# Gated linear attention into a four-expert MLP: crossbar transposes replaced by TensorE transposes, and the first gate logits loaded from ACT's queue

## The chip, the cores and the metric

One core of one Trainium2 chip. The metric is the device time of one execution in microseconds (us), as the median of several runs. Three runs of the kernel before took 315.59, 315.67 and 315.96 us.

The engines are named as in the profile: PE is TensorE (PEld its weight loads), DVE VectorE, ACT ScalarE, POOL GpSimd, and SP the engine whose queue issues most DMAs here.

## What is computed

Two stages. The first is a linear attention with a per-channel forget gate over 4 batches, 8 heads, 768 steps and 48 channels a head:

```python
f = 1.0 / (1.0 + np.exp(-f_logit))
for t in range(S):
    state = f[:, :, t, :, None] * state + np.einsum('bhd,bhe->bhde', k[:, :, t], v[:, :, t])
    y[:, :, t] = np.einsum('bhd,bhde->bhe', q[:, :, t], state)
```

The second takes y as 3072 rows of 384 values (rows by batch and step, columns by head and channel) through four experts, each 384 to 1024 to 384 with a ReLU between, and adds the experts' results with weights p, which are the domain probabilities divided by their sum:

```python
for e in range(E):
    h = np.maximum(x @ w1[e], 0.0)
    out += p[:, e:e + 1] * (h @ w2[e])
```

## The kernel before, in words

The sequence is cut into 6 chunks (c = 0 to 5) of 128 steps. For each chunk the attention is done for 4 batches (b), all 8 heads at once, and gives 4 x 128 columns of x transposed (xT); the experts then work on these 512 columns together.

**Attention of one batch of one chunk.** ACT turns the gate logits into log gates (lines 236 and 240, two steps). PE makes their running sum along the chunk with a triangular matrix (244; 247 makes the totals of the chunk). ACT takes exponentials of both signs (251, 252, 254). Q and K are multiplied with them (257, "product", on POOL or DVE) and V is cast (261). Q and K are needed with the channel on the partition, so they are transposed; how depends on the chunk:

- chunks 0 and 1: PE transposes (265, `pe_tp`): four for Q and four for K, each 112 columns wide (two heads, padded to 64 each), into PSUM, and DVE copies them to the tile QK (214).
- chunks 2 to 5: one crossbar DMA per batch from SP's queue (269, `dma_tp`), from the padded tile `qk` straight into QK.

PE then makes the scores (280), DVE masks them (284), and PE adds scores times V and, from chunk 1 on, the state's part into y (295, 291). ACT or DVE casts y to bf16 (214, tile yb). This is transposed into xT: in chunks 0 and 1 by three PE transposes (320, `pe_xt`) and a copy by ACT or DVE (212 or 214), in chunks 2 to 5 by one DMA from SP's queue (273, `dma_xt`). Except in the last chunk, PE makes K times V (301), DVE adds it to the state (308), and POOL scales the state by the chunk's gate total and casts it (315, 316).

**Experts.** An "up" group is three matmuls of 512 columns (324), followed by a ReLU on ACT or DVE (332, 330). A "down" group is four matmuls of 384 columns (336); after two of them ACT or DVE scales and adds the result to the output tile (343, 345, 347), which SP stores (351).

**What sets the order.** A small planner (class `Plan`) is given every step with the engines that can do it, a modelled cost on each, a priority, what it depends on and which buffers ("rooms") it takes and frees. It runs through modelled time and starts, on each engine that is free, the ready step of the best priority whose buffers are free. The program is written out in that order, so every engine works strictly in the planned order. Attention of chunk c + 1 is planned among the expert work of chunk c. PSUM has two rooms for up groups, two for down groups and four for everything in the attention.

**Loads.** Each batch of chunk 0 has its own load of f (gate logits), K, Q and V (192 KB each); later chunks load two batches at a time (384 KB). All are issued from SP's queue, in planned order; chunk 0's order is f0 k0 q0 f1 f2 k1 q1 v0 f3 k2 q2 v1 k3 q3 v2 v3 (line 364). The weights, eight transfers of 768 KB, are issued from POOL's queue and wait for K of batch 3 to have landed (227); the gate load that starts chunk 1 waits for the sixth weight transfer (221).

Of the kernel before, what the change touches and what calls it, by code (L numbers as in the profile page):

```python
# [9 lines left out]
BF16 = mybir.dt.bfloat16  # L10
# [87 lines left out]
def kernel(  # L98
# [11 lines left out]
    nc = tc.nc  # L110
    B, H, S, D = q.shape
    assert (B, H, S, D) == (4, 8, 768, 48)
    T = 128
    C = S // T
    HD = H * D
    NP = H // 2
    P2 = 64
    MP = P2 + D
# [5 lines left out]
    engines = {"ACT": nc.scalar, "DVE": nc.vector, "POOL": nc.gpsimd}  # L124
# [4 lines left out]
    wk = ctx.enter_context(tc.tile_pool(name="wk", bufs=1))  # L129
    PS = bass.MemoryType.PSUM  # L130
    ps = ctx.enter_context(tc.tile_pool(name="ps", bufs=1, space=PS))
    rooms = {"ps_h": 2, "ps_o": 2, "ps_t": 4, "f": 4, "q": 4, "k": 4, "v": 4, "ex": 2, "gp": 4, "e": 2, "qk": 7,
             "vb": 7, "egs": 8, "QK": 2, "AT": 2, "yb": 2, "xT": 2, "h": 2, "o": 8}
    P = Plan(rooms)

# [8 lines left out]
    ones = const.tile([T, 1], BF16)  # L144
    nc.gpsimd.memset(ones, 1.0)
    pads = {}
    for nm, nb in (("gp", 2), ("qk", 2)):
        for i in range(rooms[nm]):
            t = pads[nm, i] = const.tile([T, nb, H, P2], BF16, name=f"{nm}{i}")
            nc.vector.memset(t[:, :, :, D:P2], 0.0)  # L150
# [3 lines left out]
        out=mask01, in_=mask01, compare_op=ALU.is_ge, fill=0.0,  # L154
# [5 lines left out]
    for i in range(2):  # L160
        t = const.tile([MP, B, NP, 2 * D], BF16, name=f"sb{i}")
# [11 lines left out]
    for nm, a in (("f", f_logit), ("q", q), ("k", k), ("v", v)):  # L173
        srcs[nm] = a.rearrange("b h (c t) d -> c t (b h) d", t=T)
    ins = {}
# [1 line left out]
    shapes = {  # L177
        "f": ([T, 2 * H, D], FP32), "q": ([T, 2 * H, D], FP32), "k": ([T, 2 * H, D], FP32), "v": ([T, 2 * H, D], FP32),
        "ex": ([T, 2 * H, D], FP32), "e": ([T, 2, HD], FP32), "egs": ([MP, NP], FP32), "vb": ([T, H, D], BF16),
        "QK": ([128, 2, NP, T], BF16), "AT": ([T, 2, NP, T], BF16), "yb": ([T, HD], BF16),  # L180
        "xT": ([128, KD, NT], BF16), "h": ([128, KF, NT], BF16), "o": ([128, Din], FP32),
        "cs": ([T, 512], FP32), "tp": ([MP, 2, NP, T], BF16), "A": ([T, NP, T], FP32), "y": ([T, 512], FP32),
        "KV": ([T, 512], FP32), "xp": ([T, KD, T], BF16), "ps_h": ([128, NT], FP32), "ps_o": ([128, 512], FP32),
# [2 lines left out]
    def tl(kind, *key):  # L186

        if (kind, key) not in tiles:
            room = kind if kind in rooms else "ps_t"
            slot = P.slot[(room, kind) + key if room == "ps_t" else (room,) + key]  # L190
            if room in ("gp", "qk"):
                tiles[kind, key] = pads[room, slot]
            else:
                shape, dt = shapes[kind]
                pool = ps if room.startswith("ps_") else wk
                tiles[kind, key] = pool.tile(shape, dt, name=f"{room}{slot}")
        return tiles[kind, key]
# [6 lines left out]
    def flat(t, i):  # L204
        return t[:, 2 * i:2 * i + 2, :].rearrange("t h d -> t (h d)")

    def hh(b, n=1):
        return slice((b % 2) * H, (b % 2 + n) * H)

    def copy(eng, out, in_):  # L210
        if eng == "ACT":
            nc.scalar.copy(out=out, in_=in_)  # L212
        else:
            engines[eng].tensor_copy(out=out, in_=in_)  # L214


    def load(c, nm, b, n):
        ins[c, nm, b] = nc.sync.dma_start(out=tl(nm, c, b // 2)[:, hh(b, n), :],
                                          in_=srcs[nm][c, :, b * H:(b + n) * H, :])
        if (c, nm, b) == (1, "f", 0):  # L220
            after(ins[c, nm, b], ins["w", 5])
# [32 lines left out]
            nc.scalar.activation(out=tl("egs", c, b), in_=cs[0:MP, HD:HD + NP], func=AF.Exp, scale=-1.0)  # L254

    def product(c, b, j, eng):
        engines[eng].tensor_tensor(out=tl("qk", c, b)[:, j, :, 0:D], in0=tl("qk"[j], c, b // 2)[:, hh(b), :],  # L257
                                   in1=tl("e", c, b)[:, j].rearrange("t (h d) -> t h d", d=D), op=ALU.mult)

    def cast_v(c, b, eng):  # L260
# [1 line left out]

    def pe_tp(c, b, j):
        for i in range(NP):
            nc.tensor.transpose(out=tl("tp", c, b)[:, j, i, :], in_=flat(tl("qk", c, b)[:, j], i)[:, 0:MP],  # L265
                                identity=ident)

    def dma_tp(c, b):
        nc.sync.dma_start_transpose(out=tl("QK", c, b).rearrange("m j i t -> m (j i) t"),
                                    in_=tl("qk", c, b).rearrange("t j h d -> t (j h d)"))  # L270

    def dma_xt(c, b):
        nc.sync.dma_start_transpose(out=tl("xT", c)[:, :, b * T:(b + 1) * T], in_=tl("yb", c, b))

    def pe_at(c, b):
        QK = tl("QK", c, b)
# [10 lines left out]
    def pe_y(c, b):  # L287
        y, AT, vb, QK = tl("y", c, b), tl("AT", c, b), tl("vb", c, b), tl("QK", c, b)
        for i in range(NP):
            if c > 0:  # L290
                nc.tensor.matmul(out=y[:, i * 2 * D:(i + 1) * 2 * D], lhsT=QK[0:MP, 0, i, :],  # L291
                                 rhs=Sb[c % 2][:, b, i, :], start=True, stop=False, skip_group_check=True)
            for r in range(2):
                h = 2 * i + r
                nc.tensor.matmul(out=y[:, h * D:(h + 1) * D], lhsT=AT[:, r, i, :], rhs=vb[:, h, :],  # L295
                                 start=(c == 0), stop=True, skip_group_check=True)

    def pe_kv(c, b):
        kp, vb = tl("qk", c, b)[:, 1], tl("vb", c, b)
        for i in range(NP):  # L300
            nc.tensor.matmul(out=tl("KV", c, b)[0:MP, i * 2 * D:(i + 1) * 2 * D], lhsT=flat(kp, i)[:, 0:MP],  # L301
                             rhs=flat(vb, i), start=True, stop=True)
# [51 lines left out]
    ld = {}  # L354
    nw = [(0, 1), (1, 1), (0, 2), (2, 1), (1, 2), (3, 1), (2, 2), (3, 2)]

    def add_load(c, nm, b, n, prio, deps=()):
        op = P.add(f"ld {nm}{c}.{b}", {"DMA": 1.05 * n}, lambda e: load(c, nm, b, n), prio,
                   deps=deps, takes=[(nm, c, b // 2)], lag=2.0)
        for i in range(n):  # L360
            ld[c, nm, b + i] = op
        return op

    for i, x in enumerate("f0 k0 q0 f1 f2 k1 q1 v0 f3 k2 q2 v1 k3 q3 v2 v3".split()):
        add_load(0, x[0], int(x[1]), 1, -1000 + i)
    pload = P.add("ld p", {"DMA": 0.3}, lambda e: nc.sync.dma_start(
        out=pt, in_=moe_domain_probs.rearrange("(n p) e -> p n e", p=128)), -900, lag=2.0)
# [13 lines left out]
    def attention(c, slot, gran):  # L381
# [10 lines left out]
        for b in range(B):  # L392
# [8 lines left out]
                       takes=[("e", c, b)] + ([("egs", c, b)] if more else []), frees=[pt_("cs")])  # L401
            pe = {"POOL": 1.0, "DVE": 0.56} if c < 2 else {"POOL": 1.0}
            qm = P.add(f"q {c}.{b}", pe, one(product, 0), s(4) - 0.2,
                       deps=[ex, ld[c, "q", b]], takes=[("qk", c, b)], frees=[("q", c, half), ("e", c, b)])
            km = P.add(f"k {c}.{b}", pe, one(product, 1), s(4) - 0.1,
                       deps=[ex, ld[c, "k", b]], takes=[("qk", c, b)], frees=[("k", c, half), ("e", c, b)])
            vb = P.add(f"v {c}.{b}", {"POOL": 0.5, "DVE": 0.36} if c < 2 else {"POOL": 0.5}, one(cast_v), s(4),
                       deps=[ld[c, "v", b]], takes=[("vb", c, b)], frees=[("v", c, half)])
            if c < 2:
                tq = P.add(f"tpq {c}.{b}", {"PE": 0.22}, on(pe_tp, 0), s(4), deps=[qm],  # L410
                           takes=[pt_("tp")], frees=[("qk", c, b)], lag=0.2)
                tk = P.add(f"tpk {c}.{b}", {"PE": 0.22}, on(pe_tp, 1), s(4) + 0.01, deps=[km],
                           takes=[pt_("tp")], frees=[("qk", c, b)], lag=0.2)
                et = P.add(f"ev_tp {c}.{b}", {"DVE": 0.69}, lambda e, b=b: copy(e, tl("QK", c, b)[0:MP], tl("tp", c, b)), s(4) + 0.1,
                           deps=[tq, tk], takes=[("QK", c, b)], frees=[pt_("tp")])
            else:
                et = P.add(f"tp {c}.{b}", {"DMA": 1.8}, on(dma_tp), s(4), deps=[qm, km], takes=[("QK", c, b)],
                           frees=[("qk", c, b)], lag=2.2)
            at = P.add(f"at {c}.{b}", {"PE": 0.35}, on(pe_at), s(7), deps=[et],
                       takes=[pt_("A", 0), pt_("A", 1)], lag=0.2, frees=[("QK", c, b)])  # L420
            eA = [P.add(f"ev_at{r} {c}.{b}", {"DVE": 0.7}, on(ev_at, r), s(7) + 0.1 + 0.1 * r, deps=[at],
# [3 lines left out]
            ey = P.add(f"ev_y {c}.{b}", {"ACT": 0.48, "DVE": 0.56},  # L425
                       lambda e, b=b: copy(e, tl("yb", c, b), tl("y", c, b)[:, 0:HD]), s(11) + 0.1,
                       deps=[y], takes=[("yb", c, b)], frees=[pt_("y")])
            if c < 2:
                xt = P.add(f"xt {c}.{b}", {"PE": 0.17}, on(pe_xt), s(13), deps=[ey],
                           takes=[pt_("xp")], frees=[("yb", c, b)], lag=0.2)  # L430
                xdone[c, b] = P.add(f"ev_xt {c}.{b}", {"ACT": 0.48, "DVE": 0.4},
                                    lambda e, b=b: copy(e, tl("xT", c)[:, :, b * T:(b + 1) * T], tl("xp", c, b)),
                                    s(13) + 0.1, deps=[xt], takes=[("xT", c)], frees=[pt_("xp")])
            else:
                xdone[c, b] = P.add(f"xt {c}.{b}", {"DMA": 0.9}, on(dma_xt), s(13), deps=[ey], takes=[("xT", c)],
                                    frees=[("yb", c, b)], lag=2.2)
            if more:
                kv = P.add(f"kv {c}.{b}", {"PE": 0.22}, on(pe_kv), s(15), deps=[km, vb, y],
                           takes=[pt_("KV")], frees=[("vb", c, b), ("qk", c, b)], lag=0.2)
                ek = P.add(f"ev_kv {c}.{b}", {"DVE": 0.74}, on(ev_kv), s(15) + 0.1,  # L440
                           deps=[kv, kvdone.get((c - 1, b))], frees=[pt_("KV")])
                kvdone[c, b] = P.add(f"state {c}.{b}", {"POOL": 1.75}, on(state), s(15) + 0.2,
                                     deps=[ek, ex], frees=[("egs", c, b)])
# [106 lines left out]
```

## Time and profile before

| what | value |
|---|---|
| median of three runs | 315.67 us |
| profiled execution, its own time | 315.96 us |
| its span, first to last instruction | 314.1 us |
| mean granted TensorE clock | 1.000 |
| first expert matmul starts | 25.38 us |
| end of the last matmul | 310.2 us |
| mean DMA rate over the span | 115 GB/s |

The table's first row is what runs are compared by. The profile is of one execution, whose own time is 0.29 us above that median; its span leaves out 1.86 us around the instructions. A view of busy time by stage gives, for a stretch of the span, how long each engine was busy and how many instructions it ran. In a timeline, each row is a run of equal instructions with start and length in us; rows of PE overlap because matmuls are pipelined, so the distance from one start to the next is what a group costs in a dense stream. "Idle before" names what ended an engine's idle time.

### The profile page before, as it was taken

To read this page: it belongs to the slowest core of one execution; us is meant where nothing else is said; L and a number is where in the kernel's file an instruction comes from. 1 tells how busy PE (TensorE), PEld (TensorE's weight loads), DVE (VectorE), ACT (ScalarE), POOL (GpSimd) and SP (SyncE) were. 2 spreads that over 40 slices of the span, in tenths; PEclk is the share of its full clock that TensorE was granted. 3 is DMA by queue.
4 is the path that set the end of the run, shared out by engine and by line. 5 is a ranking of instruction groups with operands and counts; after the bars stand their busy time and mean duration, and the time that the engine had idled before them with its cause. 6 is when DMAs were issued, how large, how long until landed. Compare 5 with 4: busy or idle time off the path is not lost.

```text
span 314.1 us, 5415 instructions
## 1 busy us (share of the span) xinstructions
PE 295.3 (94%) x2098; PEld 171.1 (54%) x2128; DVE 132.5 (42%) x249; ACT 163.0 (52%) x310; POOL 92.6 (29%) x160
## 2 busy tenths in 40 slices
PE   1978999998999999999999999999999999999995
PEld 1753455556876555655555555555555555555552
DVE  6791002379954466443553222554332442201223
ACT  5634664554767563667544456443466444465430
POOL 4695000026996333860322200223322200000000
PEclk9999999999999999999999999999999999999999
DMA  8999999999999087999692113200322200200002
GB/s 156 211 150 192 196 208 201 208 202 214 189 223 236 6 172 140 230 197 189 108 196 48 50 50 48 46 15 13 95 75 46 50 13 15 75 25 2 0 0 100
DMA packets 135081, 36.05 MB, mean 115 GB/s; under 512 B 126352, under 2 KB 133520, under 8 KB 135056
## 3 DMA queue, kind: packets, MB, share of 16 engines
q1 hardware_dynamic: 129296, 29.42, 49.2%
q0 software_dynamic: 5760, 6.29, 12.0%
q8 instruction: 16, 0.26, 0.4%
q14 instruction: 9, 0.07, 0.1%
HBM read 31.51 MB, written 4.72 MB: 115 GB/s over the span
## 4 chain that ended last, share of the span: by engine, by line
PE 88%; DVE 7%; issue 2%; ACT 1%; DMA 1%; DVEq 0%; ACTq 0%
PE ps_h L324 40%; PE ps_o L336 39%; PE ps_t L280 2%; DVE qk L257 2%; DVE AT L284 2%; PE ps_t L295 1%; PE ps_t L244 1%; PE ps_t L291 1%; PE ps_t L301 1%; PE ps_t L247 1%; DMA f<-in_f_logit_dram 1%; PE ps_t L265 1%; DVE QK L214 1%; DVE o L343 1%; DVE vb L261 1%
## 5 line engine op out<-in xcount | busy, mean ns | idle before, releaser
L332 ACT ACTIVATE h<-ps_h 128x512 bf16<-128x512 f32 (+1 forms) x176 | 101.7, 579 | 111.2 <-PE ps_h L324 104.1
L324 PE MATMUL ps_h<-xT,w_sb 128*128 128x512 bf16 (+1 forms) x594 | 154.0, 367 | 2.9 <-ACT xT L212 0.6
L336 PE MATMUL ps_o<-w_sb,h 128*128 128x384 bf16 x768 | 153.0, 326 | 0.2
L336 PEld LDWEIGHTS <-h 128*128 128x128 bf16 x768 | 72.0, 98 | 56.8
L343 DVE SCALAR_TENSOR_TENSOR o<-ps_o,pn,o 128x384 f32<-128x384 f32 x72 | 44.4, 617 | 109.2 <-PE ps_o L336 101.9
L324 PEld LDWEIGHTS <-w_sb 128*128 128x128 bf16 x624 | 60.5, 99 | 50.9 <-issue 6.5
L284 DVE TENSOR_TENSOR AT<-ps_t,mask 128x512 bf16<-128x512 f32 x48 | 31.2, 684 | 14.8 <-PE ps_t L280 14.7
L261 POOL CAST vb<-v 128x384 bf16<-128x384 f32 x20 | 10.7, 537 | 72.9 <-DMA v<-in_v_dram 36.5
L257 POOL TENSOR_TENSOR qk<-q,e 128x384 bf16<-128x384 f32 x21 | 21.2, 1014 | 30.2 <-ACT e L251 29.9
L315 POOL TENSOR_TENSOR Sf<-Sf,egs 48x192 f32<-48x192 f32 x40 | 20.3, 508 | 24.6 <-DVE Sf L308 22.7
L330 DVE TENSOR_SCALAR h<-ps_h 128x256 bf16<-128x256 f32 (+1 forms) x32 | 17.4, 549 | 23.6 <-PE ps_h L324 23.2
L257 POOL TENSOR_TENSOR qk<-k,e 128x384 bf16<-128x384 f32 x19 | 19.3, 1015 | 21.8 <-ACT egs L254 11.3
L308 DVE TENSOR_TENSOR Sf<-Sf,ps_t 48x192 f32<-48x192 f32 x40 | 13.9, 349 | 10.7 <-PE ps_t L301 10.0
L251 ACT ACTIVATE e<-ps_t 128x384 f32<-128x384 f32 x24 | 11.8, 491 | 10.5 <-PE ps_t L247 4.6
L345 ACT ACTIVATE o<-ps_o,pn 128x384 f32<-128x384 f32 x22 | 12.8, 580 | 5.2 <-PE ps_o L336 4.5
L214 DVE CAST yb<-ps_t 128x384 bf16<-128x384 f32 x17 | 9.5, 556 | 13.8 <-PE ps_t L295 12.4
L316 POOL CAST sb<-Sf 48x192 bf16<-48x192 f32 x40 | 13.5, 339 | 2.6
L295 PE MATMUL ps_t<-vb,AT 128*128 128x48 bf16 x192 | 12.5, 190 | 1.5 <-DVE AT L284 1.4
L244 PE MATMUL ps_t<-gp,Ub 128*128 128x384 bf16 x24 | 8.5, 355 | 5.4 <-ACT gp L240 4.9
L295 PEld LDWEIGHTS <-AT 128*128 128x128 bf16 x192 | 10.5, 101 | 4.3 <-DVE AT L284 2.1
L252 ACT ACTIVATE e<-ps_t 128x384 f32<-128x384 f32 x24 | 11.9, 494 | 0.0
L236 ACT ACTIVATE ex<-f 128x768 f32<-128x768 f32 (+1 forms) x14 | 10.5, 753 | 1.9 <-DMA f<-in_f_logit_dram 1.7
(44 smaller groups left out, 138.7 us busy)
## 6 DMA issues: line engine op xcount, KB each, us to landing
w_sb<-in_moe_w_dram POOLq DMA_DIRECT2D x8, 768.0 KB, 20.9
out_dram<-o SPq DMA_DIRECT2D x24, 192.0 KB, 1.9
k<-in_k_dram SPq DMA_DIRECT2D x10, 384.0 KB, 5.3
f<-in_f_logit_dram SPq DMA_DIRECT2D x10, 384.0 KB, 5.6
q<-in_q_dram SPq DMA_DIRECT2D x10, 384.0 KB, 5.2
v<-in_v_dram SPq DMA_DIRECT2D x10, 384.0 KB, 5.8
f<-in_f_logit_dram SPq DMA_DIRECT2D x4, 192.0 KB, 3.9
k<-in_k_dram SPq DMA_DIRECT2D x4, 192.0 KB, 3.9
```

Source lines behind the costliest of these rows:

```text
L257: engines[eng].tensor_tensor(out=tl("qk", c, b)[:, j, :, 0:D], in0=tl("qk"[j], c, b // 2)[:, hh(b), :], in1=tl("e", c, b)[:, j].rearrange( ...
L261: engines[eng].tensor_copy(out=tl("vb", c, b), in_=tl("v", c, b // 2)[:, hh(b), :])
L284: nc.vector.tensor_tensor(out=tl("AT", c, b)[:, r].rearrange("s i t -> s (i t)"), in0=tl("A", c, b, r).rearrange("s i t -> s (i t)"), in1= ...
L295: nc.tensor.matmul(out=y[:, h * D:(h + 1) * D], lhsT=AT[:, r, i, :], rhs=vb[:, h, :], start=(c == 0), stop=True, skip_group_check=True)
L308: nc.vector.tensor_tensor(out=Sf[rows, b], in0=Sf[rows, b], in1=KV[rows, :, r, :], op=ALU.add)
L315: nc.gpsimd.tensor_tensor(out=Sf[rows, b], in0=Sf[rows, b], in1=eg, op=ALU.mult)
L316: nc.gpsimd.tensor_copy(out=nb[rows, b, :, r * D:(r + 1) * D], in_=Sf[rows, b])
L324: nc.tensor.matmul(out=tl("ps_h", c, e, fc, n0)[:, n0:n1], lhsT=w1_sb[:, e, kk, fc * 128:(fc + 1) * 128], rhs=tl("xT", c)[:, kk, n0:n1], s ...
L330: nc.vector.tensor_relu(out=dst, in_=src)
L332: nc.scalar.activation(out=dst, in_=src, func=AF.Relu)
L336: nc.tensor.matmul(out=tl("ps_o", c, e, nt)[:, 0:Din], lhsT=tl("h", c, e)[:, fc, nt * T:(nt + 1) * T], rhs=w2_sb[:, e, fc, :], start=(fc = ...
L343: nc.vector.scalar_tensor_tensor(out=o, in0=op, scalar=pe, in1=o, op0=ALU.mult, op1=ALU.add)
```

## The change

- The DMA transposes are gone. All chunks use `pe_tp` with the copy to QK, and `pe_xt` with the copy to xT.
- The padded tile `qk`, which held the products of Q and K together (7 rooms), becomes two: `qp` (6 rooms) and `kp` (7 rooms).
- The four gate-logit loads of chunk 0 are issued from ACT's queue; the planner counts each as 0.2 us of ACT, with a landing time that grows with the batch. All other loads stay on SP's queue.

Since the planner lays out the whole program anew, the order changes on every engine. In the changed program ACT's first instructions are the table load and the four gate loads; then come both gate steps of batch 0, both of batch 1, and the exponentials of batches 0 and 1. SP's order for chunk 0 is k0 q0 k1 q1 v0 k2 q2 v1 k3 q3 v2 v3. POOL makes the Q products of batches 0 and 1 and one cast of V, then issues the eight weight transfers, and then scales the states; before, it also made both products of batch 2 and scaled one state ahead of the weights. DVE makes the K products of batches 0 and 1 and both products of batches 2 and 3. The four steps that normalise the probabilities (230 to 233) stand ahead of DVE's last mask of chunk 0; before, they stood behind it. The steps of the attentions of chunks 1 and 2 stand closer together in PE's order than before.

The diff, cut to its core:

```diff
-    rooms = {..., "e": 2, "qk": 7,
+    rooms = {..., "e": 2, "qp": 6, "kp": 7,
...
-    def load(c, nm, b, n):
-        ins[c, nm, b] = nc.sync.dma_start(out=tl(nm, c, b // 2)[:, hh(b, n), :],
+    def load(c, nm, b, n, eng):
+        ins[c, nm, b] = (nc.scalar if eng == "ACT" else nc.sync).dma_start(out=tl(nm, c, b // 2)[:, hh(b, n), :],
...
-    def dma_tp(c, b):
-        nc.sync.dma_start_transpose(out=tl("QK", c, b).rearrange("m j i t -> m (j i) t"),
-                                    in_=tl("qk", c, b).rearrange("t j h d -> t (j h d)"))
-
-    def dma_xt(c, b):
-        nc.sync.dma_start_transpose(out=tl("xT", c)[:, :, b * T:(b + 1) * T], in_=tl("yb", c, b))
...
-        op = P.add(f"ld {nm}{c}.{b}", {"DMA": 1.05 * n}, lambda e: load(c, nm, b, n), prio,
-                   deps=deps, takes=[(nm, c, b // 2)], lag=2.0)
+        op = P.add(f"ld {nm}{c}.{b}", {"ACT": 0.2} if c == 0 and nm == "f" else {"DMA": 1.05 * n},
+                   lambda e: load(c, nm, b, n, e), prio, deps=deps, takes=[(nm, c, b // 2)],
+                   lag=2.0 + (1.0 + b if c == 0 and nm == "f" else 0))
...
-            if c < 2:
-                tq = P.add(f"tpq {c}.{b}", {"PE": 0.22}, on(pe_tp, 0), s(4), deps=[qm],
-                           takes=[pt_("tp")], frees=[("qk", c, b)], lag=0.2)
...
-            else:
-                et = P.add(f"tp {c}.{b}", {"DMA": 1.8}, on(dma_tp), s(4), deps=[qm, km], takes=[("QK", c, b)],
-                           frees=[("qk", c, b)], lag=2.2)
+            tq = P.add(f"tpq {c}.{b}", {"PE": 0.22}, on(pe_tp, 0), s(4), deps=[qm],
+                       takes=[pt_("tp")], frees=[("qp", c, b)], lag=0.2)
+            tk = P.add(f"tpk {c}.{b}", {"PE": 0.22}, on(pe_tp, 1), s(4) + 0.01, deps=[km],
+                       takes=[pt_("tp")], frees=[("kp", c, b)], lag=0.2)
+            et = P.add(f"ev_tp {c}.{b}", {"DVE": 0.69}, lambda e, b=b: copy(e, tl("QK", c, b), tl("tp", c, b)), s(4) + 0.1,
+                       deps=[tq, tk], takes=[("QK", c, b)], frees=[pt_("tp")])
...
-            else:
-                xdone[c, b] = P.add(f"xt {c}.{b}", {"DMA": 0.9}, on(dma_xt), s(13), deps=[ey], takes=[("xT", c)],
-                                    frees=[("yb", c, b)], lag=2.2)
+            xt = P.add(f"xt {c}.{b}", {"PE": 0.17}, on(pe_xt), s(13), deps=[ey],
+                       takes=[pt_("xp")], frees=[("yb", c, b)], lag=0.2)
+            xdone[c, b] = P.add(f"ev_xt {c}.{b}", {"ACT": 0.48, "DVE": 0.4},
+                                lambda e, b=b: copy(e, tl("xT", c)[:, :, b * T:(b + 1) * T], tl("xp", c, b)),
+                                s(13) + 0.1, deps=[xt], takes=[("xT", c)], frees=[pt_("xp")])
```

## The prediction

> **What bounds the kernel now.** I read the page first: busy times, slices, and the chain that ended last.
>
> ```profile
> PE 295.3 (94%) x2098; PEld 171.1 (54%) x2128; DVE 132.5 (42%) x249; ACT 163.0 (52%) x310; POOL 92.6 (29%) x160
> ...
> PE   1978999998999999999999999999999999999995
> ...
> PE 88%; DVE 7%; issue 2%; ACT 1%; DMA 1%; DVEq 0%; ACTq 0%
> ```
>
> PE is 88% of the chain and its slices are full from the fourth on; the holes are at the start and in the eleventh slice. Busy time by stage says how full:
>
> ```profile
> 6.59:23.17 16.58, 12.78 (x125) 10.03 (x125) 13.63 (x26) 8.62 (x22) 13.00 (x18) 1.00 1.19 181
> 64.00:84.00 20.00, 18.06 (x227) 13.43 (x226) 18.51 (x34) 11.80 (x30) 12.71 (x19) 1.00 1.17 198
> 150.00:200.00 50.00, 49.69 (x357) 27.44 (x362) 20.13 (x38) 24.13 (x41) 11.76 (x26) 1.00 0.39 77
> ```
>
> After the span come PE, PEld, DVE, ACT and POOL busy, granted clock, DMA share, GB/s. From 150 to 200 us PE idles 0.31 of 50 us, though ten of the 32 crossbar transposes fall there. From 64 to 84 us (attention of the second chunk) it idles 1.94 us while DVE is busy 18.51 of 20. In the start-up DVE has 13.6 of 16.6 us and the DMA share is above 1. So three resources matter, each in its place: DVE and the loads until the first expert matmul at 25.38, DVE again near 64 to 84, and PE everywhere else.
>
> **The transposes.** The change adds, for 16 batches (chunks 2 to 5, four each), 8 PE transposes of Q and K and 3 of x: 176 matmuls. The second chunk does exactly this today, so the trace has the price among full-speed neighbours:
>
> ```profile
> 74.00 0.33 PE L320 MATMUL ps_t<-ident,yb 128*128 128x128 bf16 x3
> 74.16 0.61 PE L265 MATMUL ps_t<-ident,qk 128*112 128x128 bf16 x8
> 74.61 0.81 PE L336 MATMUL ps_o<-w_sb,h 128*128 128x384 bf16 x4
> ...
> 75.46 0.62 PE L265 MATMUL ps_t<-ident,qk 128*112 128x128 bf16 x8
> 75.91 0.21 PE L291 MATMUL ps_t<-sb,QK 112*128 112x96 bf16 x1
> ```
>
> Durations overlap, so the price is the distance to the next start: 74.16 to 74.61 and 75.46 to 75.91, 0.45 us for eight; 74.00 to 74.16 is 0.16 for three, and 81.91 to 82.08 gives 0.17. Per batch 0.62 us, times 16: **9.9 us**, on an engine with 0.3 us in 50 to hide it in. Bounds from other rows: eight 48x128 matmuls of line 280 take 0.33 us (69.55 to 69.88), so 176 x 0.041 = 7.2 at least; the start-up's transposes, with slow neighbours, take 1.01 for eight and 0.48 for three, 23.8 at most. I take 9.9: same shape, same neighbours.
>
> The Trainium skill (TensorE: Matmul & The Clock Gate, Part 4) puts a PE transpose of 128x128 at about 275 ns inside a kernel and says its latency dominates. By that the sum would be 176 x 0.275 = 48 us; this trace starts one every 0.056 us, so I keep the row.
>
> What leaves: 32 crossbar transposes on SP's queue, 1.2 us of issue and 2.4 to 3.2 to landing each. They gave PE almost nothing to wait for:
>
> ```profile
> PEld L280 <- issue: 7.1, 17, 0.5
> ```
>
> These 7.1 us are idle time of the weight load, under running matmuls; on PE itself the step before line 280 loses 0.09 us (153.17 + 0.65 to 153.91), and the second chunk, fed by DVE, loses the same 0.09 (72.26 + 0.65 to 73.00). So nothing comes back: 0, bounded by 16 x 0.09 = 1.4. SP's loads and stores no longer queue behind those issues; the loads run well ahead by then, so 0.
>
> What arrives elsewhere: DVE gets 16 copies of QK at 0.68 (10.9 us) and xT copies are shared by ACT (0.48) and DVE (no row; its yb copy is 0.56). In the changed program's order DVE has 256 rows for 231. Past 110 us DVE is at about 40%, and 1.1 us more per batch is hidden by that slack. Between chunks 1 and 2 it is not obvious; see the second rival.
>
> **The start-up.** Chunk 0 already used PE transposes; here the order changes. The four gate loads sit on ACT's queue ahead of its first gate. No row shows an issue from ACT. Free at best; at worst they follow the table load (1.28) with SP's prices for the first four loads (0.45, 0.56, 0.82, 0.84), so the first gate starts at 0.80 + 1.28 + 2.67 = 4.8 instead of 3.76. The new order also runs both gates of batch 1 before the exponentials of batch 0. So the first K product moves from 6.59 to between 6.9 and 8.2.
>
> DVE's list then reads: K0 product, V0 cast, K1 product, two QK copies, mask 0, Q2 and K2 products, mask 1: by the steps of today's rows (1.0, 0.65, 0.81, 2 x 0.61, 1.2, 2 x 0.47, 1.2) with a few tenths of waiting 7.4 us, so at 14.3 to 15.6 it reaches the V2 cast. V2 is still the fifteenth of sixteen loads. Today:
>
> ```profile
> 12.87 1.97 SPq L218 DMA_DIRECT2D v<-in_v_dram  x2
> ...
> 17.64 0.53 DVE L261 CAST vb<-v 128x384 bf16<-128x384 f32 x1
> 18.10 1.27 DVE L284 TENSOR_TENSOR AT<-ps_t,mask 128x512 bf16<-128x512 f32 x2
> 19.29 0.55 DVE L261 CAST vb<-v 128x384 bf16<-128x384 f32 x1
> 19.76 0.67 DVE L214 COPY QK<-ps_t 112x1024 bf16<-112x1024 bf16 x1
> 20.36 1.49 DVE L308 TENSOR_TENSOR Sf<-Sf,ps_t 48x192 f32<-48x192 f32 x4
> 21.88 1.29 DVE L284 TENSOR_TENSOR AT<-ps_t,mask 128x512 bf16<-128x512 f32 x2
> ```
>
> Issued at 12.87, and 4.2 us to landing as the page has it for v: 17.1. DVE waits there, with ten groups still ahead of its last mask: V2 cast 0.47, QK copy 0.61, state sum 0.75, Q3 0.47, mask 1.19, K3 0.47, V3 cast 0.47, state sum 0.75, QK copy 0.61, state sum 0.75, and now also the four probability steps (1.14; today behind the mask): 7.7 us. The last mask starts at 24.8, today 21.88: **+2.9 us**. From that mask to the first expert matmul is the same chain as today (21.88 to 25.38). The reason is that POOL now issues the weights after two products and one cast, so that DVE has batch 2's products as well as batch 3's.
> If the loads' order on two queues brings V2 before DVE asks, the shift is 0.7; if weights, requested sooner, slow V2 by a microsecond, 3.9.
> The Trainium skill (DMA: Bandwidth & Descriptors, Issuing engines are not separate DMA queues) says that a second issuing engine saves only issue time, since all share the same 16 engines. By it V2 lands no earlier, and the shift stays 2.9; a DMA share of 1.19 agrees, but no run here shows a load issued from ACT.
>
> Weights don't stop PE: they wait for K3, still the thirteenth load, and the second chunk's K load (15.71), which competed with them, now waits behind the gate load.
>
> **Sum.** 9.9 + 2.9 + 0 elsewhere = 12.8. The profiled execution took 315.96 (span 314.1, 1.86 around it): 328.8. The shown median is 0.29 lower: **328.5**.
>
> **Rivals.**
> - *The start doesn't get later* (V2 early, or casts fill gaps). For: today DVE idles 3 us of the start-up. Against: 15th of 16 at a full DMA. Shift 0.7 to -1: 324.7 to 326.3, say 326.
> - *DVE becomes the bound while attentions 1 and 2 overlap.* In the new PE order, from about 58 to 113 us, DVE has some 40 us of work in 55, by the rows' durations. Today's loss rate, 1.94 per 20 us at 93% DVE, over all 55 is 5.3, so +3.4: 332. Against: 73% mean isn't 93%. Bounds of this term: +3.4, and -1.9 if today's hole closes.
> - *Faster: the new plan is denser than the old.* From 25.38 to 310.2 PE needs 284.8 us for work of some 276 by dense row steps (124.8 up, 124.8 down, 26 attention); 8.9 us are lost. Were all this closed, and the experts to start 3.5 earlier (V3's cast at 19.29 + 0.47 + 2.15 from last y to the first expert matmul), the change gives 9.9 - 8.9 - 3.5 = -2.5: 313.2. It decides once it saves over 10.5. Against: of the 8.9, 2.6 are the first 12 expert matmuls at 0.43 us, which any order pays.
> - *It does not do what it says:* transposes hide in PE's waits, 316 to 324; nothing at 150 to 250 us allows it.
>
> **How the numbers follow.** Forecast (326.4 to 330.5) 0.56; start not later (324 to 326.4) 0.20; DVE bound (330.5 to 333.5) 0.15; above that 0.03; transposes partly hidden (316.3 to 324) 0.03; no change 0.01; denser plan 0.02. The range 324.3 to 333 holds about 0.86. A change of 0.2% (0.6 us) is about what a measurement of this kernel can tell from none: faster 0.02, same 0.01, slower 0.97.
>
> **What would show it.** Eight transposes spaced 0.45 us in every chunk; PE busy up by about 10 us past 110; the first expert matmul near 28.3, with DVE idle before the V2 cast for a DMA; 64 to 84 us no emptier than now. Wrong if transposes cost under 7 us in the dense part, if the first expert matmul comes before 26, or if PE idles over 3 us between 58 and 113.

## The result, and the profile after

Four runs of the changed kernel took 331.55 to 334.54 us, median **332.93**; four runs of the kernel before beside them 315.22 to 315.96, median 315.63. The ratio is **1.055** (95% interval 1.050 to 1.061): slower by 17.3 us, where 12.8 were forecast. The profiled execution after is the fastest of the four (331.55), with a span of 329.8 us, 15.7 above the span before.

In the changed kernel the lines behind 265 moved: the experts' up matmul is 317 (before 324), the down matmul 329 (336), the mask 277 (284), the sum of the state 301 (308), the transpose of x 313 (320).

The page of the changed kernel, its busy times, PE's slices and granted clock, and the chain that ended last, by engine:

```profile
PE 302.1 (92%) x2273; PEld 180.2 (55%) x2304; DVE 144.4 (44%) x274; ACT 168.6 (51%) x326; POOL 89.8 (27%) x157
...
PE   1660899999999999999999999999999999999995
...
PEclk9985699999999999999999999999999999999999
...
PE 84%; DMA 7%; SPq 4%; DVE 2%; issue 1%; ACT 0%; ACTq 0%
```

PE is busier by 6.8 us, but two things are new: the fourth slice (24.7 to 33.0 us) is empty, and DMA now has 7% of the chain, where it had 1%. Busy time by stage, for the same three stretches as before (columns as there):

```profile
6.59:23.17 16.58, 11.48 (x120) 9.06 (x119) 12.44 (x23) 9.15 (x24) 10.37 (x14) 0.97 1.27 188
64.00:84.00 20.00, 19.18 (x188) 12.50 (x189) 15.87 (x27) 12.75 (x28) 8.18 (x12) 1.00 1.22 206
150.00:200.00 50.00, 49.63 (x378) 28.89 (x384) 22.75 (x41) 24.64 (x47) 14.51 (x26) 1.00 0.13 32
```

From 150 to 200 us PE is as full as before with 21 more matmuls in it, so nothing there hides them. From 64 to 84 us PE has less idle time than before, 0.82 us for 1.94; but the program is some 10 us later there, so the stretch holds other work (188 PE instructions for 227).

The empty slice is explained by two timelines. DVE in the changed kernel, at the end of the first chunk's attention (start, length, instruction, idle time before it and what ended it):

```profile
23.48 0.73 DVE L301 TENSOR_TENSOR Sf<-Sf,ps_t 48x192 f32<-48x192 f32 x2
30.77 0.25 DVE L230 TENSOR_REDUCE psm<-pt 128x24 f32<-128x96 f32 x1 [6.55 <-DMA pt<-in_moe_domain_probs_dram]
31.05 0.18 DVE L231 TENSOR_SCALAR psm<-psm 128x24 f32<-128x24 f32 x1
31.26 0.30 DVE L232 RECIPROCAL psm<-psm 128x24 f32<-128x24 f32 x1
31.60 0.26 DVE L233 TENSOR_TENSOR pn<-pt,psm 128x96 f32<-128x96 f32 x1
31.89 1.29 DVE L277 TENSOR_TENSOR AT<-ps_t,mask 128x512 bf16<-128x512 f32 x2
```

and PE behind it:

```profile
32.64 0.22 PE L288 MATMUL ps_t<-vb,AT 128*128 128x48 bf16 x1 [8.52 <-DVE AT L277]
...
35.39 0.59 PE L317 MATMUL ps_h<-xT,w_sb 128*128 128x512 bf16 x1 [0.57 <-ACT xT L212]
```

DVE is free at 24.2 us. The next instruction in its order needs the domain probabilities (tile pt), and their load has not landed; DVE waits 6.55 us, with the last mask behind it in the same queue, and PE waits for the mask. The DMA issues up to 40 us say what happened to that load (48 KB; the last number is the time from issue to landing). Before:

```profile
w_sb<-in_moe_w_dram POOLq DMA_DIRECT2D x8, 768.0 KB, 20.9
...
pt<-in_moe_domain_probs_dram SPq DMA_DIRECT2D x1, 48.0 KB, 5.8
```

After:

```profile
w_sb<-in_moe_w_dram POOLq DMA_DIRECT2D x8, 768.0 KB, 19.2
...
pt<-in_moe_domain_probs_dram SPq DMA_DIRECT2D x1, 48.0 KB, 16.3
```

It was issued earlier than before and took 16.3 us for 5.8. One thing that changed beside it is when the weights were asked for. Before:

```profile
14.88 0.78 SPq L366 DMA_DIRECT2D pt<-in_moe_domain_probs_dram  x1
16.32 6.76 POOL L225 DMA_DIRECT2D w_sb<-in_moe_w_dram  x8
```

After:

```profile
14.46 0.95 SPq L360 DMA_DIRECT2D pt<-in_moe_domain_probs_dram  x1
15.14 6.77 POOL L225 DMA_DIRECT2D w_sb<-in_moe_w_dram  x8 [0.69 <-DMA k<-in_k_dram]
```

The first weight transfer came 1.44 us behind the load before, and 0.68 behind it after.

**The account.** I cut the span at two points: the start of the first expert matmul, and the start of the last down matmul. Before: 25.4, and 284.5 us from there to 309.9. After: 35.4, and 290.3 us to 325.7. So the start gives +10.0 and the part behind it, "the long part" from here on, +5.8.

### The profile page after: what moved, and what is told of

It reads as the page before. It is cut to its first block, busy times and chain, and to the rows that moved or that the text cites. A ratio compares the mean times of both kernels' runs of the same rounds, so it can differ in the third digit from the quotient of the medians.

```text
span 329.8 us, 5754 instructions
## 1 busy us (share of the span) xinstructions
PE 302.1 (92%) x2273; PEld 180.2 (55%) x2304; DVE 144.4 (44%) x274; ACT 168.6 (51%) x326; POOL 89.8 (27%) x157
## 3 DMA queue, kind: packets, MB, share of 16 engines
q1 hardware_dynamic: 101584, 22.86, 35.5%
## 4 chain that ended last, share of the span: by engine, by line
PE 84%; DMA 7%; SPq 4%; DVE 2%; issue 1%; ACT 0%; ACTq 0%
PE ps_o L329 37%; PE ps_h L317 37%; DMA pt<-in_moe_domain_probs_dram 5%; SPq L218 4%; PE ps_t L265 2%; PE ps_t L273 2%; DMA v<-in_v_dram 2%; PE ps_t L288 1%; PE ps_t L313 1%; PE ps_t L284 1%; PE ps_t L244 1%; DVE AT L277 1%; PE ps_t L294 1%; PE ps_t L247 1%; DVE o L336 1%
## 5 line engine op out<-in xcount | busy, mean ns | idle before, releaser
L329 PE MATMUL ps_o<-w_sb,h 128*128 128x384 bf16 x768 | 155.0, 326 | 0.4 <-DVE o L336 0.2
L329 PEld LDWEIGHTS <-h 128*128 128x128 bf16 x768 | 71.2, 98 | 52.7 <-issue 0.4
L257 POOL TENSOR_TENSOR qp<-q,e 128x384 bf16<-128x384 f32 x19 | 19.3, 1017 | 41.7 <-ACT e L251 35.6
L257 POOL TENSOR_TENSOR kp<-k,e 128x384 bf16<-128x384 f32 x18 | 18.3, 1017 | 32.9 <-ACT egs L254 32.8
L323 DVE TENSOR_SCALAR h<-ps_h 128x512 bf16<-128x512 f32 (+1 forms) x31 | 17.7, 578 | 16.7 <-PE ps_h L317 11.8
L214 DVE COPY QK<-ps_t 112x1024 bf16<-112x1024 bf16 x24 | 16.5, 687 | 14.5 <-PE ps_t L265 14.5
L212 ACT CAST yb<-ps_t 128x384 bf16<-128x384 f32 x15 | 7.2, 479 | 18.1 <-PE ps_t L288 18.0
L251 ACT ACTIVATE e<-ps_t 128x384 f32<-128x384 f32 x24 | 11.8, 491 | 5.1 <-issue 2.8
L265 PE MATMUL ps_t<-ident,kp 128*112 128x128 bf16 x96 | 10.3, 234 | 2.4 <-DVE kp L257 2.4
```

The lines of the kernel that those rows point to most:

```text
L257: engines[eng].tensor_tensor(out=tl(("qp", "kp")[j], c, b)[:, 0, :, 0:D], in0=tl("qk"[j], c, b // 2)[:, hh(b), :], in1=tl("e", c, b)[:, j] ...
L323: nc.vector.tensor_relu(out=dst, in_=src)
L329: nc.tensor.matmul(out=tl("ps_o", c, e, nt)[:, 0:Din], lhsT=tl("h", c, e)[:, fc, nt * T:(nt + 1) * T], rhs=w2_sb[:, e, fc, :], start=(fc = ...
```

## Experiments

The theories. **A**: the excess of the start is the wait for the probabilities. A1, on why that load is late: the weights' transfers slow it. For the long part: the transposes cost their spacing on PE, and something in the new plan gives time back (theory C: the planner's costs for the second chunk's products). Rivals stand with each run. The kernel before was run again beside the experiments: its median was 315.19 us beside e1, e3, e4 and e5, 315.20 beside e2, e6, e7 and e8, and 315.82 beside e10 to e13; ratios are to these.

**e1: the changed kernel, probability steps behind the last copy of x.**

```diff
+    pdone.deps.append(xdone[0, B - 1])
```

> The changed kernel with one edit: the four probability steps on DVE are planned after chunk 0's attention, as in the kernel before; nothing else is moved in chunk 0. Theory A (the 6.5 us that DVE waits for the probabilities to land, in front of the last mask, are what made the start late beyond the forecast): the last mask starts near 24.2 instead of 31.9, the first expert matmul at 24.2 + 3.5 = 27.7 instead of 35.4, so 7.7 us less, about 325; up to 4 us of it may be given back where attention 1 waits for its loads, which then have less lead: 324 to 329. Rival B (the start is late because of the gate loads on ACT's queue and DVE's longer list, and the wait is only the last of several that end together): the first expert matmul stays after 32 and the time above 330.

Measured 323.16 us, ratio 1.025 (1.022 to 1.028): 9.8 us of the 17.3 are gone. DVE:

```profile
23.67 1.29 DVE L277 TENSOR_TENSOR AT<-ps_t,mask 128x512 bf16<-128x512 f32 x2
25.92 0.73 DVE L301 TENSOR_TENSOR Sf<-Sf,ps_t 48x192 f32<-48x192 f32 x2 [0.97 <-PE ps_t L294]
29.71 0.25 DVE L230 TENSOR_REDUCE psm<-pt 128x24 f32<-128x96 f32 x1 [3.05 <-DMA pt<-in_moe_domain_probs_dram]
```

The load is as late as in the changed kernel (15.3 us from issue), and DVE still waits for it, but now nothing that PE needs stands behind. The first expert matmul is at 27.2, and the long part takes 290.5. Theory A holds.

**e3: the changed kernel in its own order; the first weight transfer waits until the probabilities have landed.**

```diff
+        ins["p"] = nc.sync.dma_start(out=pt, in_=moe_domain_probs.rearrange("(n p) e -> p n e", p=128))
...
+    after(ins["w", 0], ins["p"])
```

> The changed kernel in its own order, with one wait added: the first weight transfer, and so all eight on POOL's queue, waits until the probabilities have landed. Theory A1 (the probabilities, issued at 14.5, land only at 30.8 because the weights' transfers, issued from 15.1, take the DMA engines from them): they land 5 to 7 us after their issue, near 20, as before the change; DVE doesn't wait, the last mask starts near 25.4 and the first expert matmul near 28.9; 326, or a few us more if the weights, now 5 us later, make an expert matmul wait. Rival A2 (they are slow by themselves, or because of the V loads ahead of them on SP's queue): they land near 30 again, the weights 10 us after that, and the time is above 340.

Measured 325.18 us, ratio 1.032 (1.029 to 1.034). The DMA issues up to 40 us:

```profile
pt<-in_moe_domain_probs_dram SPq DMA_DIRECT2D x1, 48.0 KB, 4.7
```

Nothing but the weights' time (and that of the state steps behind them on POOL) was changed, and the load takes 4.7 us. So A1 holds: the 768 KB transfers were what slowed it. The last mask comes at 24.53, the first expert matmul at 28.0, and the long part takes 291.1 us. The other runs agree. In the eight with the weights asked for 0.3 to 0.7 us behind this load it took 14.5 to 21.7 us (16.3 after, 21.7 in e11), in the four with them 1.2 to 1.4 us behind, 5.6 to 7.0. Those four also have all gate loads on SP's queue, so these rows alone wouldn't show that the distance decides.

**e4: the kernel before, with only the gate loads on ACT's queue** (the `load` and `add_load` lines of the change).

> The kernel before with only the gate loads of chunk 0 moved to ACT's queue; the crossbar transposes stay. Its planned order has the probability steps ahead of the last mask, as the changed kernel has. Theory A: the start is as late as in the changed kernel (first expert matmul near 35 instead of 25.4, +10), and about 4 us come back where attention 1 no longer waits for its loads: about 322. Rival (the added PE transposes are the whole loss, the loads move costs about nothing): 315 to 317.

**e5: the changed kernel, with the gate loads back on SP's queue in their old places,** so that only the transposes are changed.

> The changed kernel with the gate loads of chunk 0 back on SP's queue in the old order; all transposes on PE. Here the probability steps are planned behind the last mask. Theory A: the start is that of the kernel before (first expert matmul near 25.4) and the transposes cost 16 x 0.62 = 9.9: 325.5; with the hole of the second chunk's attention (about 4 us) closed or not, 321.5 to 326. Rival (PE transposes cost less than their spacing, since they fill holes): 316 to 320. Rival (they cost more, through new waits for DVE's copies): above 328.

e4 took 323.13 us, ratio 1.026 (1.020 to 1.032), its four runs spread over 321.54 to 325.49; e5 took 323.45, ratio 1.026 (1.024 to 1.028). Their two parts beside those of before and after:

| kernel | gate loads | transposes | first expert matmul | long part |
|---|---|---|---|---|
| before | SP | crossbar | 25.4 | 284.5 |
| e4 | ACT | crossbar | 33.5 | 282.1 |
| e5 | SP | PE | 25.1 | 292.6 |
| after | ACT | PE | 35.4 | 290.3 |

In the long part the two halves of the change add up: the transposes cost 8.1 us with either set of loads, and the plan that comes with the loads on ACT saves 2.3 to 2.4 with either kind of transpose. The late start comes with the loads: e4 has the wait too, 4.74 us ahead of the probability steps, with the load 14.5 us from issue to landing, and e5 has not. That e4's first expert matmul comes sooner than the changed kernel's (33.55 for 35.39) goes with its load landing sooner: DVE's wait for it ends at 28.92 for 30.77.

**e6: e1 with the eight Q and K transposes of chunks 2 to 5 made twice,** into the same place; the plan stays that of e1.

```diff
-        for i in range(NP):
+        for i in [*range(NP)] * (2 if c >= 2 else 1):
```

> The kernel with the probability steps last (323.2 us), with the eight PE transposes of Q and K in chunks 2 to 5 each made twice into the same PSUM tile; the plan and everything else stay as they were. If PE's own spacing is the price (0.45 us for eight, nothing hides it), 16 x 0.45 = 7.2 us more: 330.4. If PE has slack that takes in a fifth of such work (8.1 us measured for 9.9 of transposes), 5.9 more: 329. If transposes are mostly hidden: under 326.

Measured 330.45 us, ratio 1.048 (1.047 to 1.050), 7.29 over e1. For 16 x 8 transposes that is 0.057 us each; the prediction's row gave 0.056. So here, on a PE without gaps, an added transpose costs its whole distance from start to start.

**e8: e4 with the probability steps last.**

> The kernel before (crossbar transposes) with the gate loads on ACT's queue and the probability steps planned after chunk 0's attention: what the loads move is worth without the wait for the probabilities. First expert matmul near 27.2, as with all transposes on PE (25.4 before), so +1.8; after that point up to 2.3 us less than before (282.2 instead of 284.5, if that gain comes from the plan and not from the late start) : 314.7 to 317. Rival (the 2.3 us came from the start being 8 us later, with the loads of the second chunk then further ahead): 317.

Measured 315.12 us, ratio 0.9995 (0.9985 to 1.0006): no difference to before that can be measured. The first expert matmul is at 27.6, the long part takes 281.7. So the shorter long part doesn't need the late start (2.2 us of it are left, and the long part is the shortest yet); it comes with the plan. Against e1, which differs by the transposes and the order that the planner makes of them, the transposes cost 323.16 - 315.12 = **8.04 us**.

**e7: the kernel before, with the planner's costs of the second chunk's products and casts raised towards the traced ones.**

```diff
-            pe = {"POOL": 1.0, "DVE": 0.56} if c < 2 else {"POOL": 1.0}
+            pe = {"POOL": 1.0, "DVE": 0.56} if c < 1 else {"POOL": 1.1, "DVE": 0.85} if c < 2 else {"POOL": 1.0}
```

(and in the same way the casts of V, 0.6 on POOL and 0.7 on DVE).

> The kernel before with the planner's costs of the second chunk's products and V casts set to what the trace shows while DVE and POOL both work on them (POOL 1.1 and 0.6, DVE 0.85 and 0.7, for 1.0 and 0.5, 0.56 and 0.36). Theory C (the loss near 65 to 85 us, some 4 us against dense spacing, is PE waiting for products that the plan has too early): PE meets fewer waits there, 312 to 314. Rival (DVE simply has more work there than fits, whatever the order): 315 to 316.

Measured 315.09 us, ratio 1.0000 (0.9988 to 1.0011); the long part takes 283.8. Theory C isn't confirmed: these costs are not what makes the old plan the longer one.

**e2: the changed kernel, with the probabilities as the first load on SP's queue.**

```diff
-        out=pt, in_=moe_domain_probs.rearrange("(n p) e -> p n e", p=128)), -900, lag=2.0)
+        out=pt, in_=moe_domain_probs.rearrange("(n p) e -> p n e", p=128)), -1001, lag=2.0)
```

> The changed kernel with the probabilities loaded first of all on SP's queue, in place of last; the planner then puts their four steps at the head of DVE's list. By theory A no wait for them is left in front of the last mask, and the first expert matmul comes at 27 to 28.5: 322.5 to 325. A cost of the small transfer at the head (its issue was 0.8 to 1.0 us) would delay the first K and Q by up to 1 us, which DVE's later wait for V hides or not. Rival B (other causes of the late start): above 329.

Measured 326.53 us, ratio 1.036 (1.035 to 1.038), a miss. The load lands in 5.2 us, but all that follows is late; ACT's start in this kernel:

```profile
0.82 5.61 ACTq L218 DMA_DIRECT2D f<-in_f_logit_dram  x4
6.48 0.52 ACT L236 ACTIVATE ex<-f 128x384 f32<-128x384 f32 x1 [4.40 <-DMA pt<-in_moe_domain_probs_dram]
```

The four gate issues take ACT's queue 5.61 us for 4.10, until 6.43; the first gate comes right behind them, at 6.48 for 4.98. (The row names the landing of the probabilities, but that was at 6.0, and the gate's own load landed at 5.1, 4.3 us after its issue.) The first expert matmul is at 29.4, 1.4 behind e3, where the load is as quick without being first.

**e12 and e13: e8 with only one kind of transpose moved to PE,** those of x (e12) or those of Q and K (e13).

```diff
-            if c < 2:
+            if c < 6:
```

(once at the transposes of x, once at those of Q and K).

> The kernel before with the gate loads on ACT's queue and the probability steps last (315.12), and of the crossbar transposes only those of x replaced by PE transposes; those of Q and K stay with the crossbar. All transposes together cost 8.04 net at equal start, where the spacing gave 7.2 for Q and K and 2.7 for x. Theory P (the missing 1.9 us belong to both kinds in proportion): x alone costs 2.2, so 317.3. Theory X (Q and K cost their full 7.2, since doubling them did, and the crossbar path of x had cost PE some waiting): x alone costs 0.8, so 315.9. Theory Q (the waiting was on the crossbar path of Q and K): x costs its full 2.7, so 317.8.

> The counterpart: only the transposes of Q and K of chunks 2 to 5 are moved to PE, those of x stay with the crossbar. Theory P: 5.8 on top of 315.12, so 320.9. Theory X: 7.2, so 322.3. Theory Q: 5.3, so 320.4. If this and the run with x alone don't add up to 8.0, the plan makes the difference, not the transposes.

e12 took 317.59 us, ratio 1.006 (1.004 to 1.008), 1.8 us over the kernel before (1.3 to 2.5 by the interval). e13 took 321.25, ratio 1.017 (1.015 to 1.019), 5.4 over (4.8 to 6.1). The sum, 7.2, is a little under 8.04; counted from e8's 315.12, which the theories start from, it is 2.5 and 6.1, in all 8.6. Of the three theories on record, the one that put the discount on both kinds in proportion (2.2 and 5.8) lies in both intervals; the one with the full 7.2 for Q and K lies in neither, the one with the full 2.7 for x in one. That speaks against a full price for Q and K. Whether x is discounted too isn't settled: 2.5 is as near to 2.7 as to 2.2.

Where does one see it? All PE records of the up matmuls are there in e11 (below, all crossbar), e12, e13 and e1 (all PE). From 84 to 150 us, where the crossbar is first used, PE idles 0.80 us in e11, 0.47 in e12, 0.04 in e13 and 0.00 in e1. That is 0.8 of the 1.9; the rest I couldn't find as idle time. Nor does a wait name the crossbar: in e11 the waits listed for that stretch are two of 0.2 us for a ReLU on DVE. So whether the crossbar's latency cost PE the 1.9 us, or the order that the planner makes around it, stays open.

**e10: the kernel before, with all four loads of the second chunk's first half waiting for the sixth weight transfer;** before, only the first of them, the gate load, does, and the K load is issued early.

```diff
-            add_load(1, nm, 2 * half, 2, -400 + 4 * half + j, deps=[wd[5]] if half == 0 and j == 0 else [])
+            add_load(1, nm, 2 * half, 2, -400 + 4 * half + j, deps=[wd[5]] if half == 0 else [])
```

> The kernel before, with all four loads of the second chunk's first half waiting for the sixth weight transfer, as its gate load does now; today its K load is issued early (15.71 us), among the weights. The start should stay at 25.4 us or come a few tenths sooner. If the early K load is what makes the plan of the overlapping attentions worse by the 2.3 to 2.8 us that the kernels with gate loads on ACT save there (281.7 from the first expert matmul to the last down group, against 284.5), this gives 313. If not: 315.2, as before.

Measured 340.71 us, ratio 1.077 (1.074 to 1.080). The edit changed the plan in another way than meant. PE in this kernel:

```profile
21.20 0.48 PE L320 MATMUL ps_t<-ident,yb 128*128 128x128 bf16 x3
41.92 0.48 PE L244 MATMUL ps_t<-gp,Ub 128*128 128x384 bf16 x1 [20.24 <-ACT gp L240]
...
43.87 0.52 PE L320 MATMUL ps_t<-ident,yb 128*128 128x128 bf16 x3
45.29 8.89 PE L324 MATMUL ps_h<-xT,w_sb 128*128 128x512 bf16 x30 [0.89 <-DVE xT L214]
```

The gate sum of the second chunk (41.92) now stands ahead of the last transposes of the first (43.87), and it needs a gate load that waits for six weight transfers: 20.24 us of waiting. Whether the early K load is what lengthens the old plan was not answered by this. It is the same fault as in the changed kernel, three times as large.

**e11: e8 with the gate loads of batches 0 and 1 alone on ACT's queue,** those of batches 2 and 3 in their old places on SP's.

```diff
-        op = P.add(f"ld {nm}{c}.{b}", {"ACT": 0.2} if c == 0 and nm == "f" else {"DMA": 1.05 * n},
+        op = P.add(f"ld {nm}{c}.{b}", {"ACT": 0.2} if c == 0 and nm == "f" and b < 2 else {"DMA": 1.05 * n},
```

> Crossbar transposes; gate loads of batches 0 and 1 only on ACT's queue, those of batches 2 and 3 in their old places on SP's; probability steps last. ACT's sequencer then spends about 2 us less on issuing ahead of its first gate (about 3.9 us instead of 4.98). If the start follows the first gate: first expert matmul about 1 us sooner than with four (26.6 for 27.6), and 314.1 with the plan's 281.7 after it. If the start follows the landing of V2 and DVE's list: no change, 315.1. Rival, the plan of the later part goes back to the old one: 284.5 after the start, so 317.

Measured **313.97 us, ratio 0.994 (0.993 to 0.996)**: the one version that beats the kernel before, by 1.8 us. The first expert matmul comes at 26.4 for e8's 27.6, and the long part takes 282.2. Both numbers are near those of the first theory, but by luck, for its step failed: ACT's issues take 1.23 us for 4.10, and the first gate still gains only 0.18 us (4.80 for 4.98). DVE reaches its last mask at 22.86 for 24.12, in another order of its steps; which of these matters wasn't followed. Its stretch from 64 to 84 us shows where that plan gains on the old one:

```profile
64.00:84.00 20.00, 19.73 (x239) 14.66 (x238) 18.90 (x36) 12.58 (x31) 12.39 (x21) 1.00 1.05 198
```

PE idles 0.27 us there (0.27 in e8 too), 1.94 before, at about the same DVE load (18.90 for 18.51 of 20). So a busy DVE alone does not empty this stretch; the order decides. That is 1.7 us, most of the 2.3 (e11) to 2.8 (e8) between the plans. What in the planner picks the better order isn't settled, since e7 and e10, made to find it, did not.

## Why the prediction was wrong

The step that failed is the start: +2.9 us was forecast, +10.0 measured, since the probability steps were put ahead of the last mask at the price of their own length, and nothing was put down for the arrival of their load. The sign and the larger term were right, the sum too small by 4.4 us against the median: 332.93 is at the very end of the range (333.0) and outside the case that the forecast stood for (326.4 to 330.5). That it isn't further off is luck: the start was 7.1 us worse than forecast, the transposes 1.8 and the long part's plan 2.3 better. By its steps:

- **Transposes, +9.9: the price was right, the net was 8.1.** In the changed kernel, timeline of PE in the third chunk's attention:

```profile
103.31 0.33 PE L313 MATMUL ps_t<-ident,yb 128*128 128x128 bf16 x3
103.48 0.81 PE L329 MATMUL ps_o<-w_sb,h 128*128 128x384 bf16 x4
104.13 0.39 PE L265 MATMUL ps_t<-ident,qp 128*112 128x128 bf16 x4
104.35 0.39 PE L265 MATMUL ps_t<-ident,kp 128*112 128x128 bf16 x4
104.58 0.36 PE L294 MATMUL ps_t<-vb,kp 128*112 128x96 bf16 x4
```

  0.45 us for eight and 0.17 for three, as forecast, and e6 confirms that the spacing is the marginal price. The sub-step "what leaves gave PE almost nothing to wait for" (0, bounded by 1.4) was too small: 1.8 to 1.9 came back (9.9 less 8.1 or 8.04), 0.8 of it seen as idle time of PE, the rest not traced to a cause.

- **The start, +2.9: this step failed.** Its list of DVE's work was right, and in e3, where the same order runs without the wait, the first expert matmul is at 28.0 (28.3 forecast), +2.6. The V2 cast came at 17.12 (17.1 forecast), but not for the reason given. DVE in the changed kernel:

```profile
11.06 0.36 DVE L261 CAST vb<-v 128x384 bf16<-128x384 f32 x1 [1.57 <-DMA v<-in_v_dram]
...
15.91 1.29 DVE L277 TENSOR_TENSOR AT<-ps_t,mask 128x512 bf16<-128x512 f32 x2
17.12 0.80 DVE L261 CAST vb<-v 128x384 bf16<-128x384 f32 x1
```

  DVE was to reach that cast at 14.3 to 15.6 and wait for V2. It waited for V0 instead (6.7 us from issue to landing, 3.9 before), reached the cast at 17.1 by its own work, and V2 had landed at 16.8. So the agreement at this point is luck. What decided the start is another thing: the step counted the four probability steps, now ahead of the mask, as 1.14 us of DVE work, and took their load as landed. It quoted their new place and never asked when their operand arrives. The row was there: issued at 14.88 and 5.8 us to landing, so 20.7, 3.5 us ahead of the 24.2 at which DVE now asks. That looked like room enough, but the same paragraph had POOL ask for the weights sooner, and it checked only V2 against them, not the small load queued just behind V2. The load landed 10.1 us later than it did before (30.77 for 20.7), DVE waited 6.55, and the start moved by 10.0 instead of 2.9: 7.4 from the wait (35.4 less e3's 28.0; DVE stood idle for 6.55 of it and came to the wait 0.8 later than in e3) and 2.6 from the list.

- **"0 elsewhere": it was -2.3.** The new plan narrows the hole from 64 to 84 us, by 1.1 us in the changed kernel (0.82 for 1.94) and by 1.7 in e8 and e11; the rest wasn't located. The prediction had this as the lower bound of its second rival's term (-1.9), and chose 0.

- **The rivals.** *Start not later*: no, with four loads on ACT the list alone costs 2 us or so (e1, e8). *DVE becomes the bound*: no; the time fell where this rival put it, near the upper end of the range, but by a wait at the start; from 58 to 113 us PE idled 0.97 us, less than before (2.77). *Denser plan*: the mechanism exists, 2.3 to 2.8 us, far short of the 10.5 from which it would have decided. *Transposes hidden*: no.

- **The median.** By the profiled spans the change costs 15.7, by the medians 17.3. The four runs after spread over 3.0 us and those of e4 over 4.0, those of e1 and e3 over 0.9 and 0.7; only the first two have the wait on the path. That suggests that the landing of the small load varies from run to run and the profile shows an early one, and from kernel to kernel it does vary, from 14.5 to 21.7 us; no profile of a slower execution of the changed kernel was taken to show it.

- **Two readings** of PE's slices were one off: the slices are full from the fifth on, and the hole is in the tenth. Nothing rests on them.

The Trainium skill (DMA: Bandwidth & Descriptors, Issuing engines are not separate DMA queues) was cited for a second issuing engine saving only issue time, as all share the same engines. V2 agrees roughly: it landed at 16.8 us (issued at 12.64, 4.1 to landing) for 17.2 before (12.87, 4.4). The runs add that the issue time falls on the engine that issues, ahead of its own work. ACT in the changed kernel, and then in e11 with two issues:

```profile
0.83 4.10 ACTq L218 DMA_DIRECT2D f<-in_f_logit_dram  x4
4.98 0.52 ACT L236 ACTIVATE ex<-f 128x384 f32<-128x384 f32 x1 [2.90 <-DMA f<-in_f_logit_dram]
```

```profile
0.82 1.23 ACTq L218 DMA_DIRECT2D f<-in_f_logit_dram  x2
4.80 0.52 ACT L236 ACTIVATE ex<-f 128x384 f32<-128x384 f32 x1 [2.73 <-DMA f<-in_f_logit_dram]
```

The first gate, at 3.76 before, comes behind the four issues, which end at 4.93. But they cost it only 0.2 us or so: its own load had landed at 4.7 (3.9 us from issue, 2.9 before), and in e11, with the issues over at 2.05, the gate still waits for it until 4.80. Only in e2 do the issues cost much: the gate comes 1.4 us after its load has landed. The prediction's worst case of 4.8 was about right in time, though it put the whole delay on the table load and the issues.

## What to carry to other kernels

When a step moves ahead of another in an engine's order, price its operands' arrival and not only its own length: follow each input back to its transfer, and ask what else the change sends at that moment. A small late load that nobody needs soon is harmless until something critical is queued behind its consumer; keep such consumers last (e1 took back 9.8 us with one added dependence), and check it in the written order, since a planner with modelled landing times will not see it. On an engine without gaps an added instruction costs its distance from start to start, but the net can be smaller, as here by 1.9 us of 9.9: the operation it replaces, or the order planned around it, may have cost the engine a little too, spread so thin that the waits in the trace don't name it.

## What was not expected of the hardware

- A 48 KB load of 3072 rows of 16 bytes took 4.7 us from issue to landing with no weight transfers (e3), 5.8 with the weights asked for 1.44 us behind it (before), 16.3 with them 0.68 us behind it (after), and 21.7 with them 0.46 us behind it (e11). As the first load of its queue it made the first gate 1.5 us later (e2 against after).
- The first expert matmuls run at half pace, in one kernel with a clock record of full speed and in the other with one of half. Busy time by stage around the first expert matmul, before:

```profile
25.40:30.70 5.30, 5.08 (x12) 1.90 (x13) 0.00 (x0) 1.80 (x4) 3.11 (x8) 1.00 1.21 190
30.80:34.50 3.70, 3.62 (x16) 1.50 (x15) 0.00 (x0) 2.88 (x5) 0.00 (x0) 1.00 1.22 193
```

  and after:

```profile
35.40:39.20 3.80, 3.58 (x9) 1.36 (x10) 0.00 (x0) 1.20 (x2) 0.98 (x3) 0.51 1.26 209
39.30:43.00 3.70, 3.66 (x19) 1.65 (x17) 0.00 (x0) 2.60 (x5) 0.00 (x0) 1.00 1.19 207
```

  12 matmuls in 5.30 us and 9 in 3.80, so one in 0.43 us (the distance from start to start), and then one in 0.22. The granted clock (the third number from the end) is 1.00 through all of the first and 0.51 in the second.
